# Row tile 0 of x loaded in two row halves on two queues, and one early weight piece moved to the other queue

## The chip, the cores and the metric

One core of a Trainium2 chip runs the program. The metric is the device time of one execution in microseconds (us); the profile's span is about 2 us shorter. Executions at the full granted TensorE clock (0.999 to 1.000) count as fast.

## The reference, cut to what matters

```python
x = A_x                                   # 1 x 2048 x 640, bf16
xn = layernorm(x)
s = attention(xn @ wq, last 512 keys and values of the caches) @ wo     # 32 heads of 192
g = silu((silu(xn @ w_gate) * (xn @ w_up)) @ w_down)                    # F = 1536
return x + s * g
```

Only the first operations matter here: the layer norm of the first row tiles (128 rows each) and their products with `w_gate` and `w_up`.

## The kernel before

The kernel begins with loads, while TensorE (PE) runs filler matmuls on zeros, meant to raise its clock. A row tile goes x, statistics (VectorE), root (ScalarE), normalise (VectorE), transpose (PE), evacuation (ScalarE), then matmuls with the first 384 columns of both weights. These columns come in four early pieces: gate piece 0 and up piece 0 (rows of contraction blocks 0 and 1, 192 KB each), gate piece 1 and up piece 1 (blocks 2 to 4, 288 KB each).

```python
def load_x(t, eng=nc.sync):
    x_t[t] = lnx.tile([P, D], bf, name="x_t")
    eng.dma_start(out=x_t[t][:], in_=x2[t * P : (t + 1) * P, :])

def load_first(cs):
    for w_sb, w in ((wg_sb, B_w_gate), (wu_sb, B_w_up)):
        src = w[cs.start * P : cs.stop * P, 0:FQ].rearrange("(c p) f -> p c f", p=P)
        nc.sync.dma_start(out=w_sb[:, cs, 0:FQ], in_=src)
...
load_x(0, nc.scalar)
load_x(1, nc.scalar)
load_first(slice(0, 2))
load_first(slice(2, NC))
nc.scalar.activation(act_t[:], one_t[:], ACT.Sqrt)     # brings the table load forward
load_x(2)
load_x(3)
load_gu(1)
load_gu(2)
...
keep_warm(9)          # filler: 9 matmuls of 512 columns
keep_warm(6, P)       # and 6 of 128
...
ln_stats(0)
ln_sqrt(0)
ln_stats(1, lambda: ln_apply(0, (slice(0, 2 * P), slice(2 * P, D))))
ready(0)              # transposes and evacuation of tile 0
...
if t == 0:            # tile 0: pieces 0 first, then gate piece 1, then up piece 1
    order = order[:12] + [(f, s, [c]) for s in range(2) for c in range(2, NC) for f in range(3)]
```

The softmax here doesn't subtract the row's maximum and nothing guards it: scores larger than these inputs give would overflow.

## Time and profile before

| | before |
|---|---|
| median of three executions | 920.98 us (920.62 to 921.85) |
| span of the profiled one | 919.2 us |
| PE busy | 913.1 us |
| statistics of x tile 0 begin | 3.70 us |
| transposes of tile 0 begin | 5.79 us |
| first useful matmul | 6.64 us |
| last early piece (up piece 1) has landed | 2.25 + 4.8 = 7.05 us |

Read it thus: PE is the bound from its first useful matmul on, so whatever this change does is decided before about 8 us. A landing is worked out here as the start of the issue plus the profile's time from issue to landing. The prediction below shows the lines.

For comparing starts I use one **mark**: the start of the first 128x512 gate matmul, when PE has finished the four single row tiles. In the kernel before it is here (start, length, engine, line, operation):

```profile
14.76 1.24 PE L279 MATMUL gu<-xnT,wg_sb 128*128 128x512 bf16 x4
```

### The profile page before, as it was taken

The numbers are of one execution on the slowest core, as the hardware profiler recorded it, in microseconds if no ns is written. First come the engines' busy times: TensorE is split into PE (matmuls) and PEld (weight loads), VectorE is DVE, ScalarE is ACT, GpSimd is POOL, SyncE is SP. The second block draws the span as 40 slices with busy tenths as digits, with TensorE's granted clock in tenths as the row PEclk, the third lists the DMA queues.
The fourth block names the chain that finished last, engine by engine and source line by source line (L and its number), as shares of the span: only waits on it lengthen the run. The fifth ranks groups of instructions, "written<-read, shape, count | busy, mean of one in ns | idle before, by whom it ended". The sixth has DMA issues, their size and how long they took to land.

```text
span 919.2 us, 23149 instructions
## 1 busy us (share of the span) xinstructions
PE 913.1 (99%) x9898; PEld 550.9 (60%) x9920; DVE 601.7 (65%) x844; ACT 474.5 (52%) x840; POOL 85.5 (9%) x269
## 2 busy tenths in 40 slices
PE   9999999999999999999999999999999999999998
PEld 6444444465757575756565666666666666665565
DVE  6443321467677777777777777676867777777657
ACT  4222222557464646565656565655555555556471
POOL 0000000000000000000000000000000000002976
PEclk9999999999999999999999999999999999999999
DMA  9312430045353534253534353435243544343526
GB/s 310 68 35 64 90 84 0 1 75 112 54 113 50 112 49 108 55 107 55 108 58 109 57 109 54 108 53 105 59 82 78 90 77 80 85 71 102 121 58 166
DMA packets 248150, 77.53 MB, mean 84 GB/s; under 512 B 228976, under 2 KB 248048, under 8 KB 248048
## 3 DMA queue, kind: packets, MB, share of 16 engines
q1 hardware_dynamic: 246032, 73.67, 39.3%
q10 hardware_dynamic: 2016, 2.39, 0.8%
q8 instruction: 77, 1.26, 0.6%
q14 instruction: 25, 0.20, 0.1%
HBM read 38.93 MB, written 2.62 MB: 45 GB/s over the span
## 4 chain that ended last, share of the span: by engine, by line
PE 99%; issue 0%; DVE 0%; ACT 0%
PE mm L447 22%; PE sc L461 18%; PE mm L486 16%; PE sc L601 15%; PE sc L279 11%; PE mm L309 6%; PE sc L571 4%; PE sc L563 2%; PE mm L538 2%; PE mm L563 1%; PE gu L227 1%; PE gu L279 0%; PE mm L318 0%; PE sc L486 0%; PE sc L538 0%
## 5 line engine op out<-in xcount | busy, mean ns | idle before, releaser
L465 ACT ACTIVATE p_t<-sc 128x1024 bf16<-128x1024 f32 x254 | 253.0, 1023 | 119.9 <-PE sc L461 119.9
L452 DVE TENSOR_REDUCE qT<-mm 128x512 bf16<-128x1024 f32 x189 | 231.1, 1223 | 99.0 <-PE mm L447 96.6
L516 ACT ACTIVATE O_b<-mm,r 128x192 bf16<-128x192 f32 x486 | 165.1, 422 | 183.7 <-issue 139.7
L447 PE MATMUL mm<-xnT,wq_p 64*128 64x512 bf16 x1890 | 237.7, 376 | 0.0
L461 PE MATMUL sc<-qT,khat 64*128 64x512 bf16 x1524 | 198.1, 376 | 0.0
L486 PEld LDWEIGHTS <-p_t 64*128 64x128 bf16 x3584 | 159.6, 93 | 33.6
L486 PE MATMUL mm<-V_p,p_t 64*128 64x193 bf16 x3520 | 176.8, 242 | 0.0
L614 DVE TENSOR_TENSOR s_m<-s_m,sc 128x1024 f32<-128x1024 f32 x108 | 131.9, 1221 | 60.4 <-PE sc L601 52.3
L601 PE MATMUL sc<-wo_p,OT_b 64*128 64x512 bf16 x1296 | 168.9, 376 | 0.0
L447 PEld LDWEIGHTS <-wq_p 64*128 64x128 bf16 x1890 | 105.8, 94 | 98.1 <-issue 0.8
L461 PEld LDWEIGHTS <-khat 64*128 64x128 bf16 x1536 | 85.9, 94 | 79.9 <-DVE s_t L614 0.3
L601 PEld LDWEIGHTS <-OT_b 64*128 64x128 bf16 x1296 | 70.5, 94 | 43.8 <-issue 0.3
L614 DVE TENSOR_TENSOR s_t<-s_t,sc 128x512 f32<-128x512 f32 x108 | 74.2, 687 | 28.4 <-PE sc L571 26.6
L588 POOL MEMSET turn_t<- 128x1 f32 x220 | 21.8, 99 | 700.0 <-PE mm L486 506.0
L287 DVE TENSOR_TENSOR hT<-sc,sg 128x512 bf16<-128x512 f32 x46 | 31.7, 692 | 81.6 <-ACT sg L286 81.6
L286 ACT ACTIVATE sg<-sc 128x512 bf16<-128x512 f32 x46 | 27.3, 597 | 69.8 <-PE sc L279 65.1
L279 PE MATMUL sc<-xnT,wg_sb 128*128 128x512 bf16 (+1 forms) x255 | 60.0, 354 | 0.4
L279 PE MATMUL sc<-xnT,wu_sb 128*128 128x512 bf16 (+1 forms) x255 | 59.5, 355 | 0.2
L571 PE MATMUL sc<-OT_b,wo_p 64*128 64x512 bf16 (+1 forms) x345 | 50.3, 376 | 0.0
L309 PE MATMUL mm<-wd_sb,hT 128*128 128x512 bf16 x189 | 43.6, 379 | 0.2
L279 PEld LDWEIGHTS <-wu_sb 128*128 128x128 bf16 x285 | 27.1, 98 | 26.9 <-issue 0.2
L279 PEld LDWEIGHTS <-wg_sb 128*128 128x128 bf16 x285 | 27.2, 98 | 26.4
(83 smaller groups left out, 418.1 us busy)
## 6 DMA issues: line engine op xcount, KB each, us to landing
wo_p<-in_A_wo_dram SPq DMA_DIRECT2D x16, 480.0 KB, 4.8
K_p<-in_A_k_cache_dram SPq DMA_DIRECT2D x32, 192.0 KB, 4.3
V_p<-in_A_v_cache_dram SPq DMA_DIRECT2D x32, 192.0 KB, 3.3
wq_p<-in_A_wq_dram SPq DMA_DIRECT2D x64, 80.0 KB, 2.9
wq_p<-in_A_wq_dram SPq DMA_DIRECT2D x16, 160.0 KB, 3.2
x_t<-in_A_x_dram SPq DMA_DIRECT2D x14, 160.0 KB, 2.8
x_b<-in_A_x_dram SPq DMA_DIRECT2D x4, 512.0 KB, 6.1
OT_b<-O_b SPq DMA_TRANSPOSE x124, 2.8
```

Of the source, the lines that this page charges most:

```text
L279: nc.tensor.matmul(out, w_sb[:, c, f * P : (f + 1) * P], xnT[:, c, qc], start=(c == 0), stop=(c == NC - 1),)
L287: nc.vector.tensor_tensor(hTs[b][:, f, :], u, sg[:], ALU.mult)
L309: nc.tensor.matmul(dn, at, by, start=(f == 0), stop=(f == NF - 1))
L447: nc.tensor.matmul(q_ps[:, h, :], pairs[pr]["wq"][r, c, j * P : (j + 1) * P], xnT[r, c, b * 512 : (b + 1) * 512], start=(c == 0), stop=(c ...
L452: nc.vector.reduce_sum(qTs[i][:, j, :], q_ps[:, :, :].rearrange("p h n -> p n h"), axis=AX.X)
L461: nc.tensor.matmul(sc[:, h, :], khat[r, j, ks], qT[r, j, :], start=(j == 0), stop=(j == 2))
L465: nc.scalar.activation(p_t[:, :, :], sc[:, :, :], ACT.Exp, scale=scale)
L486: m = nc.tensor.matmul(acc[:, k, h * 256 : h * 256 + Dh + 1], Ps[i][kc][r, h, qt * P : (qt + 1) * P], V_p[r, kc, h, 0 : Dh + 1], start=(p ...
L516: nc.scalar.activation(O_b[:, qt, h, :], a_k[:, h, 0:Dh], ACT.Copy, scale=r[:, k, h, :])
L571: nc.tensor.matmul(ps.rearrange("p (t q) -> p t q", q=P), pairs[i // NB]["wo"][r, j, MC:D], OTs[i][:, :, :].rearrange("p (t j) q -> p j t ...
L601: m = nc.tensor.matmul(ps[:, k, :], OTs[i][r, 3 * (2 * half + k) + j, :], pairs[i // NB]["wo"][r, j, MAIN], start=(turn == 0 and j == 0), ...
L614: nc.vector.tensor_tensor(to, to, ps, ALU.add)
```

## The change

The intent: row tile 0, which everything waits for at the start, should land earlier if each queue carries half of its rows. To relieve SyncE's queue of what it now carries, up piece 1 goes to ScalarE's queue, ahead of the Sqrt table load.

```diff
-        def load_x(t, eng=nc.sync):
+        def load_x(t, engs=(nc.sync,)):
             x_t[t] = lnx.tile([P, D], bf, name="x_t")
-            eng.dma_start(out=x_t[t][:], in_=x2[t * P : (t + 1) * P, :])
+            n = P // len(engs)
+            for k, eng in enumerate(engs):
+                r = slice(k * n, (k + 1) * n)
+                eng.dma_start(out=x_t[t][r, :], in_=x2[t * P + r.start : t * P + r.stop, :])
...
-                nc.sync.dma_start(out=w_sb[:, cs, 0:FQ], in_=src)
+                eng.dma_start(out=w_sb[:, cs, 0:FQ], in_=src)
...
-        load_x(0, nc.scalar)
-        load_x(1, nc.scalar)
+        load_x(0, (nc.scalar, nc.sync))
+        load_x(1, (nc.scalar,))
         load_first(slice(0, 2))
-        load_first(slice(2, NC))
+        load_first(slice(2, NC), (nc.sync, nc.scalar))
```

More of the change, by code (lines that the diff above doesn't have):

```diff
@@ L181, with load_first @@
         x_t, ln, xns = {}, {}, {}
-        def load_x(t, eng=nc.sync):
+        def load_x(t, engs=(nc.sync,)):
             x_t[t] = lnx.tile([P, D], bf, name="x_t")
-            eng.dma_start(out=x_t[t][:], in_=x2[t * P : (t + 1) * P, :])
-        def load_first(cs):
-            for w_sb, w in ((wg_sb, B_w_gate), (wu_sb, B_w_up)):
+            n = P // len(engs)
+            for k, eng in enumerate(engs):
+                r = slice(k * n, (k + 1) * n)
+                eng.dma_start(out=x_t[t][r, :], in_=x2[t * P + r.start : t * P + r.stop, :])
+        def load_first(cs, engs=(nc.sync, nc.sync)):
+            for w_sb, w, eng in zip((wg_sb, wu_sb), (B_w_gate, B_w_up), engs):
                 src = w[cs.start * P : cs.stop * P, 0:FQ].rearrange("(c p) f -> p c f", p=P)
-                nc.sync.dma_start(out=w_sb[:, cs, 0:FQ], in_=src)
+                eng.dma_start(out=w_sb[:, cs, 0:FQ], in_=src)
         def load_gu(q):
```

## The prediction

> **What bounds the kernel now.** I read the page first, then busy time by stretch, then the start in order of time, then the packets of the two DMA queues. The page says that TensorE (PE) is the bound.
>
> ```profile
> span 919.2 us, 23149 instructions
> PE 913.1 (99%) x9898; PEld 550.9 (60%) x9920; DVE 601.7 (65%) x844; ACT 474.5 (52%) x840; POOL 85.5 (9%) x269
> PE 99%; issue 0%; DVE 0%; ACT 0%
> ```
>
> Only 6.1 us of the 919.2 have no matmul in flight, and the chain that ended last runs along PE alone. So a change counts only if it lets PE begin its real work earlier or takes a gap out of its stream. The table of stretches says where such time lies (columns: stretch, length, then busy us and count of PE, PEld, DVE, ACT, POOL, the clock, DMA share, GB/s):
>
> ```profile
> 0.00:20.00 20.00, 18.66 (x179) 12.67 (x181) 12.02 (x36) 9.24 (x20) 0.79 (x8) 1.00 0.97 304
> 20.00:100.00 80.00, 79.63 (x365) 36.22 (x371) 33.52 (x70) 20.90 (x35) 3.81 (x6) 1.00 0.29 66
> 900.00:919.20 19.20, 15.50 (x100) 9.43 (x98) 13.50 (x24) 1.53 (x5) 11.76 (x9) 0.98 0.64 183
> ```
>
> The change touches the first ten microseconds only. There PE is idle 20.00 - 18.66 = 1.34 us, of which 1.23 us pass before its first instruction. But "busy" covers filler: 15 matmuls on zeros. The timeline of the start shows when real work begins:
>
> ```profile
> 0.71 0.91 ACTq L185 DMA_DIRECT2D x_t<-in_A_x_dram  x2
> 0.72 0.46 SPq L190 DMA_DIRECT2D wg_sb<-in_B_w_gate_dram  x1
> 1.66 1.28 ACT L205 ACT_TABLE_LOAD   x1 [1.66 <-PEq L841]
> 3.70 0.89 DVE L240 BATCH_NORM_STATS2 stats<-x_t 128x6 f32<-128x320 bf16 x2 [2.52 <-DMA x_t<-in_A_x_dram]
> 4.75 0.44 DVE L240 BATCH_NORM_STATS2 stats<-x_t 128x6 f32<-128x320 bf16 x1
> 5.19 0.16 DVE L262 RECIPROCAL rstd<-rstd 128x1 f32<-128x1 f32 x1
> 5.39 0.34 DVE L264 TENSOR_SCALAR xn<-x_t,mv,rstd 128x256 bf16<-128x256 bf16 x1
> 5.58 0.31 PE L227 MATMUL gu<-zero_t 128*128 128x128 bf16 x1
> 5.79 0.13 PEld L332 LDWEIGHTS <-xn 128*128 128x128 bf16 x2 [0.17 <-DVE xn L264]
> 6.22 0.37 ACT L338 COPY xnT<-tp 128x256 bf16<-128x256 bf16 x1 [1.06 <-PE tp L332]
> 6.64 0.27 PE L279 MATMUL sc<-xnT,wg_sb 128*128 128x128 bf16 x1
> ```
>
> The reader is to see one chain: row tile 0 of x lands at 3.70, VectorE sums it, ScalarE takes the root, VectorE normalises, and PE transposes at 5.79 after a wait of 0.17 for xn. The evacuation follows at 6.22 and the first useful matmul at 6.64. The last filler matmul starts at 5.58. Fillers of this shape are spaced 0.11 us (5.47 to 5.58), so PE would be free at 5.69: **the late x costs PE only 5.79 - 5.69 = 0.10 us.** That is the figure on which everything below turns.
>
> **What the Trainium skill says.** (1) "DMA: Bandwidth & Descriptors", Rules for kernel authors, advises against two transfers to disjoint partition halves: both halves use all 16 DMA engines and share them. The same page, Issuing engines are not separate DMA queues, says a second issuing engine saves only issue time. The trace agrees for a loaded machine (about 340 to 370 GB/s from 2.8 us on, whichever queue the packets are from), but not for the first half microsecond: between 1.8 and 2.2 us ScalarE's queue (q10) moved only 134 to 138 GB/s with its engines shown 88 to 100% occupied, and the rate rose when the other queue (q1) joined. (2) "ScalarE: Activation LUTs", What ACT_TABLE_LOAD costs, gives about 1.28 us per load plus a drain; the trace has 1.28 us, and the next ACTIVATE follows at 2.95, so no drain shows. (3) "TensorE: Matmul & The Clock Gate", Part 1, says that the array starts at half clock and goes to full only after some microseconds of activity, in a free-running window. The trace agrees: small matmuls are 0.11 us apart until about 7.0 us and 0.055 us after.
>
> **The change part by part.** *Row tile 0 in two halves.* Before, 160 KB go on q10. Both ScalarE loads make 288 packets in this window, so 144 a tile. The counts per 0.2 us from 1.6 are 5, 21, 21, 25, 25, 18, 20, 25: 144 is reached near 3.1 us, and the tile lands (issue 0.71 + 3.0) at 3.70. A half is 72 packets, and q10 reached 5 + 21 + 21 + 25 = 72 at 2.4 us. The other half leads on q1, whose first packets came near 2.1 us; at q10's 25 per 0.2 us it ends near 2.7. With the same 0.6 us from last packet to landing, x lands between 3.0 and 3.4 (an estimate): **0.3 to 0.7 us earlier.**
>
> *Row tile 1.* It matters because VectorE runs in order, and one statistics half of tile 1 (4.75 to 5.19) stands ahead of the reciprocal of tile 0. It lands at 1.17 + 3.4 = 4.57 now. It follows 72 packets in place of 144, so I expect 4.0 to 4.4. The reciprocal then starts near 4.5 to 4.9, and the first part of xn is ready 0.20 + 0.34 us later, at 5.0 to 5.4. That is before 5.69, so **the filler becomes the limit**, and only 0.10 of the 0.3 to 0.7 us reaches PE.
>
> *What 0.10 us at the transposes is worth.* First useful matmul at 6.54 in place of 6.64. But the clock rises near 7.0 us by its own window, and before that a matmul takes 0.11 in place of 0.055 us. If that instant stays, the 0.10 us hold one slow matmul more and save one fast one: 0.055 us. If it moves along: 0.10. I take 0.08 us.
>
> *SyncE's queue starts one x half (some 0.46 us of issue) later.* Gate piece 0 lands at 0.72 + 3.4 = 4.1 and would land near 4.5; up piece 0 at 1.24 + 3.9 = 5.1, then 5.5 to 5.9; both are first used at 6.6. Gate piece 1 lands at 1.74 + 4.4 = 6.1; all early bytes (320 KB of x, 960 KB of weights) are in at 7.05 now, so even as the last of them it comes by about 7.05, and its first weight load is at 7.44 (7.34 if all moves up). Hidden, with a margin of 0.3 us in the worst case.
>
> *The last up piece on ScalarE's queue.* Lands at 2.25 + 4.8 = 7.05 now, first used at 7.94. Issued near 1.6 it lands near 6 to 6.6. Already hidden: nothing gained, nothing lost.
>
> *Table load.* Three issues of some 0.44 us from 0.71 end near 2.1 in place of 1.62, so load and dummy Sqrt end near 3.65 in place of 3.15. The first real Sqrt is at 4.86, perhaps 4.3 afterwards. Hidden.
>
> *x tiles 2 and 3.* Same five issues ahead of tile 3 on SyncE, so about the same landing (7.5 and 7.9) against their use at 7.89 and 8.93.
>
> Sum: -0.08 us of 921.
>
> **The rivals.** (a) The split brings nothing because both halves share engines, as the first page says: 0.0 us. For it: the full rate later on. Against it: the slow first half microsecond. (b) A weight becomes PE's wait, because the weights now share the engines with twice as many queues: gate piece 1 past 7.35 would cost 0.1 to 0.5 us, so 921.1 to 921.5. For it: DMA share is 1.0 from 3 us on. Against: the margins above; I give it one in seven. (c) The whole chain moves up: if the clock rises during the filler, the filler ends early, and x sets PE's start with all its 0.3 to 0.7 us: 920.3 to 920.7. This trace has the filler slow to its end; one in seven. (d) A later consumer gives the gain back: the ScalarE evacuations leave only gaps of 0.1 us (10.79 to 10.97), and these move with PE, so I don't expect it.
>
> **Range and chances.** Centre 920.98 - 0.08 = 920.9 us. The three runs before span 920.62 to 921.85, so the scatter of 1.2 us is fifteen times the effect; the clock's free phase could make such scatter, which this one trace can't show. Range 920.0 to 921.8. A change by 2% is 18.4 us, more than twice all that lies before the first useful matmul: faster 0.005, same 0.99, slower 0.005.
>
> **What would show it.** Right: the first statistics start at 3.0 to 3.4; the wait of PEld for xn at the first transposes is gone and they start at 5.69; first useful matmul near 6.54; later matmuls in the same spacing; table load near 2.1. Wrong: the statistics still at 3.6 or later (rival a); weight loads on wg_sb waiting for a DMA near 7.4 (rival b); fillers at 0.055 us before 5.5 (rival c). The number fails if the executions of the new kernel fall on another part of the scatter than those of the old one.

## The result, and the profile after

The changed kernel takes 921.21 us (median of 6, 920.99 to 921.87); the kernel before, run beside it, 921.25 us (median of 6, 920.62 to 922.26). The ratio is 0.9999 with a 95% interval of 0.9986 to 1.0012: the same. (The ratio is the mean time of the one kernel's fast runs over that of the other's in the same rounds, so not quite the ratio of the medians.)

The page's lines, and the table of stretches:

```profile
span 919.0 us, 23151 instructions
PE 99%; DMA 1%; SPq 0%; issue 0%; DVE 0%
0.00:20.00 20.00, 18.45 (x179) 12.14 (x181) 12.19 (x36) 9.21 (x20) 0.79 (x8) 1.00 0.95 297
20.00:100.00 80.00, 79.63 (x366) 36.29 (x371) 33.52 (x70) 20.90 (x35) 3.81 (x6) 1.00 0.30 68
```

After 20 us nothing changed: 79.63 us of PE busy in the second stretch, as before. Before 20 us PE is busy 0.21 us *less* (18.45 against 18.66) although the mark comes 0.08 us earlier. And the chain that ended last, which was PE to the start before, now holds DMA. The timeline of the start, with the same instructions as in the prediction:

```profile
0.72 0.60 SPq L188 DMA_DIRECT2D x_t<-in_A_x_dram  x1
0.72 1.20 ACTq L188 DMA_DIRECT2D x_t<-in_A_x_dram  x2
1.38 0.81 SPq L193 DMA_DIRECT2D wg_sb<-in_B_w_gate_dram  x1
2.24 0.45 SPq L193 DMA_DIRECT2D wu_sb<-in_B_w_up_dram  x1
2.43 1.28 ACT L208 ACT_TABLE_LOAD   x1 [2.43 <-issue]
3.42 0.89 DVE L243 BATCH_NORM_STATS2 stats<-x_t 128x6 f32<-128x320 bf16 x2 [2.24 <-DMA x_t<-in_A_x_dram]
5.51 0.63 PE L335 MATMUL tp<-ident,xn 128*128 128x128 bf16 x5
6.26 0.22 PE L282 MATMUL sc<-xnT,wg_sb 128*128 128x128 bf16 x1
6.54 0.10 PEld L282 LDWEIGHTS <-wu_sb 128*128 128x128 bf16 x1 [0.52 <-DMA wu_sb<-in_B_w_up_dram]
7.40 0.28 PEld L282 LDWEIGHTS <-wg_sb 128*128 128x128 bf16 x5 [0.25 <-DMA wg_sb<-in_B_w_gate_dram]
```

The statistics of x begin 0.28 us earlier, the transposes start 0.28 us earlier, the first useful matmul 0.38 us earlier. Then PE stops twice: for up piece 0, and for gate piece 1. (The weight loads wait 0.52 and 0.25 us; the starts of the matmuls around them are 0.28 and 0.30 us apart in place of 0.055, so PE itself loses 0.23 and 0.24.) Neither wait exists in the kernel before, where SyncE issues these two pieces 1.00 us earlier, at 1.24 and 1.74 in place of 2.24 and 2.74:

```profile
1.24 0.46 SPq L190 DMA_DIRECT2D wu_sb<-in_B_w_up_dram  x1
1.74 0.46 SPq L190 DMA_DIRECT2D wg_sb<-in_B_w_gate_dram  x1
```

From issue to landing (the last number, us; first the kernel before, then the changed one) they take 0.4 and 0.2 us longer:

```profile
wu_sb<-in_B_w_up_dram SPq DMA_DIRECT2D x1, 192.0 KB, 3.9
wg_sb<-in_B_w_gate_dram SPq DMA_DIRECT2D x1, 288.0 KB, 4.4
```

```profile
wu_sb<-in_B_w_up_dram SPq DMA_DIRECT2D x1, 192.0 KB, 4.3
wg_sb<-in_B_w_gate_dram SPq DMA_DIRECT2D x1, 288.0 KB, 4.6
```

The chain of the changed kernel's execution names the second wait as the one that counts: a transfer issued at 2.74 ends PE's wait at 7.41.

```profile
2.24 0.45 SPq L193
2.69 0.04 issue
2.74 4.62 DMA wg_sb<-in_B_w_gate_dram
7.36 0.05 issue
7.41 0.28 PE sc L282 x2
```

Part of the early start is not of the change at all. In this execution the clock rose near 5.1 us (from there the fillers start 0.056 us apart in place of 0.107), so the filler ended early; in the profiled execution of the kernel before it rose near 7.0.

### The profile page after: what moved, and what is told of

Same layout as the page of the kernel before. It is cut to its first block, busy times and chain, and to the rows that moved or that the text cites. A ratio compares the mean times of both kernels' runs of the same rounds, so it can differ in the third digit from the quotient of the medians.

```text
span 919.0 us, 23151 instructions
## 1 busy us (share of the span) xinstructions
PE 912.8 (99%) x9898; PEld 548.4 (60%) x9920; DVE 601.6 (65%) x844; ACT 474.4 (52%) x840; POOL 85.5 (9%) x269
## 4 chain that ended last, share of the span: by engine, by line
PE 99%; DMA 1%; SPq 0%; issue 0%; DVE 0%
PE mm L450 22%; PE sc L464 18%; PE mm L489 16%; PE sc L604 15%; PE sc L282 11%; PE mm L312 6%; PE sc L574 4%; PE sc L566 2%; PE mm L541 2%; PE mm L566 1%; DMA wg_sb<-in_B_w_gate_dram 1%; PE gu L282 0%; PE mm L321 0%; PE sc L541 0%; PE sc L489 0%
```

## The experiments

Twelve runs, on several chips. A look is one execution with its profile; each line gives the statistics of tile 0 ("x"), the landings of up 0, gate 1 and up 1, the sum of weight loads' waits for transfers, and the mark.

| run | x | up 0 | gate 1 | up 1 | waits | mark |
|---|---|---|---|---|---|---|
| before, first look | 3.70 | 5.1 | 6.1 | 7.05 | 0 | 14.76 |
| b_again | 3.60 | 4.9 | 6.55 | 7.35 | 0 | 14.53 |
| b_third | 3.66 | 5.2 | 6.15 | 7.05 | 0 | 14.44 |
| after, first look | 3.42 | 6.5 | 7.35 | 5.85 | 0.77 | 14.68 |
| a_again | 3.47 | 6.35 | 7.55 | 5.75 | 0.9 | 14.88 |
| split_only | 3.44 | 6.15 | 7.95 | 8.8 | 1.0 | 15.93 |
| move_only | 3.79 | 5.2 | 7.85 | 6.95 | 0.6 | 15.17 |
| halves_act | 5.78 | 4.6 | 6.85 | 7.85 | 0 | 16.57 |
| cols_split | 3.08 | 7.3 | 8.2 | 7.5 | 1.9 | 15.52 |
| up_act | 3.41 | 5.95 | 8.6 | 9.0 | 1.2 | 15.94 |
| up_act_whole | 3.53 | 7.55 | 5.6 | 8.8 | 1.1 | 15.52 |
| cols_only | 3.00 | 5.2 | 6.1 | 7.6 | 0.2 | 14.85 |
| cols_f8 | 3.12 | 5.2 | 6.1 | 7.4 | 0 | 14.54 |
| cols_x2 | 2.97 | 5.6 | 7.4 | 8.2 | 0.3 | 14.99 |

One caution on the landings. The packed trace holds sixteen completion signals for each load, and the profile's landing is the last of them. In the five looks at the two kernels themselves, the last signal of an early weight piece comes at most 0.24 us after the fifteenth. In five of the other looks it comes 0.4 to 1.2 us after it, and there the fifteenth came before PE needed the piece (needed: 0.055 us after the start of the last matmul before it; all in us):

| look | piece waited for | 15th signal | last signal | needed |
|---|---|---|---|---|
| split_only | gate 1 | 6.93 | 7.92 | 7.24 |
| up_act | gate 1 | 7.42 | 8.60 | 7.47 |
| up_act_whole | up 0 | 6.47 | 7.55 | 6.89 |
| cols_only | up 1 | 7.18 | 7.62 | 7.44 |
| cols_x2 | up 1 | 7.36 | 8.18 | 7.94 |

So these waits hang on one signal of sixteen in a single look. Whether its lag belongs to the program or to the execution is not shown. Where it matters I also give the eighth signal, by which half of the signals are in.

The theory at the outset: x is early as intended, and its half on SyncE's queue delays the weights behind it. The rival: the moved up piece takes the bandwidth from them.

### Both kernels again: what belongs to an execution

No edit.

> The kernel before, unchanged, for a second look at what differs between executions of one program. If the TensorE clock rises at an instant that belongs to the execution (free window), the spacing of the filler matmuls falls from 0.11 to 0.055 us at another time than near 7.0 us. Landings should repeat: row tile 0 summed from 3.6 to 3.8, no weight load waits for a DMA, first useful matmul 6.4 to 6.7. If instead the early clock belongs to the changed kernel, this run rises near 7.0 again.

> The changed kernel, unchanged. If its two waits for weights (0.52 us for up piece 0, 0.25 us for gate piece 1) belong to the program, they are here again within 0.2 us each, the statistics of tile 0 start at 3.3 to 3.6, and the transposes of tile 1 start at 8.0 to 8.2. If they were an accident of that execution, no weight load waits for a DMA and those transposes start before 7.8.

> A third look at the kernel before, to know the scatter of its start. As in the first two looks: x summed at 3.5 to 3.8, no weight load waits for a transfer, the clock rises anywhere between 4.5 and 7.1 us, the mark at 14.4 to 14.9, later with a later rise.

The waits belong to the program: a_again has both, and neither further look at the kernel before has any. Their sizes moved by more than the 0.2 us forecast, though (gate piece 1: 0.58 us against 0.25). From a_again's list of waits (engine, line, what it waited for, us in all, times, longest):

```profile
PEld L282 <- DMA wg_sb<-in_B_w_gate_dram: 0.6, 1, 0.6
PEld L282 <- DMA wu_sb<-in_B_w_up_dram: 0.3, 1, 0.3
```

The clock does not. A 128x128 matmul is recorded at 0.31 us while the clock is low and at 0.22 when it is up. In the kernel before, first look, they fall to 0.22 near 7.1 us; in b_again the last filler, at 5.58, is already at 0.24, and in b_third the clock is up before that. A late rise goes with a mark 0.2 to 0.3 us later in the kernel before (14.76 against 14.53 and 14.44). So the first-look comparison, 14.76 to 14.68, sets a late clock against an early one. **Where both had an early clock, the changed kernel's mark is later, by 0.15 to 0.44 us** (14.68 and 14.88 against 14.53 and 14.44). Against b_third the sum closes within 0.02 us: the first useful matmul comes 0.24 and 0.20 us earlier (6.26 and 6.30 against 6.50), PE then loses 0.47 and 0.62 us to the two waits, and the mark is 0.24 and 0.44 us later. Four looks are few, and the size is not settled. The time cannot help: all 28 executions of the kernel before in this study average 921.16 us, the 7 of the changed one 921.33, with standard deviations of 0.46 and 0.36 us.

### One part at a time

split_only:

```diff
-        load_first(slice(2, NC), (nc.sync, nc.scalar))
+        load_first(slice(2, NC))
```

> Tile 0 in halves on the two queues, last up piece left on SyncE. Theory (the half on SyncE's queue delays the weights behind it): up piece 0 is waited for again, by 0.3 to 0.6 us, and x is summed at 3.3 to 3.5. Rival (the moved up piece takes bandwidth from the weights): no wait for up piece 0 and gate piece 1, as the moved piece is away. In either case the last up piece lands later than in the changed kernel.

move_only:

```diff
-        load_x(0, (nc.scalar, nc.sync))
+        load_x(0, (nc.scalar,))
```

> Tile 0 whole on ScalarE's queue, last up piece moved there. Theory (the half on SyncE is the cause): SyncE issues its first gate piece at 0.72 and up piece 0 at 1.24 as in the kernel before, no weight load waits, x is summed at 3.6 to 3.8, first useful matmul at 6.5 to 6.7. Rival (the moved piece is the cause): a wait of 0.2 us or more for up piece 0 or gate piece 1.

Neither the theory nor its rival holds alone: **each part by itself makes gate piece 1 late**, at 7.95 with the split alone and 7.85 with the move alone, against 6.1 to 6.55 before. So say the eighth signals too: 6.22 and 6.68, against 5.51 to 5.82 before and 6.79 and 7.04 with both parts. From the issue to that signal it is 3.47 us with the split alone, 4.93 with the move alone, 3.77 to 4.07 before, and 4.05 and 4.30 with both (one or two looks each, three before). So the split delays the piece by its later issue, and the move alone by a longer transfer; in the changed kernel the later issue, 1.00 us, is most of it. With the split alone, up piece 0 was not waited for (it landed at 6.15, and this execution's late clock put its first use at 6.57), so that expectation missed. Gate 1, up 1 and x tile 2 were waited for instead (gate 1 through its last signal alone, see the caution above), and its single time was 922.35 us beside 920.96 for the kernel before. With the move alone SyncE issues as early as before, and still:

```profile
PEld L282 <- DMA wg_sb<-in_B_w_gate_dram: 0.6, 1, 0.6
```

Here up piece 1 no longer comes after gate piece 1 but beside it, on the other queue, and the x tiles behind move up. By the landings one would say that, given the split, the move helps (gate piece 1 at 7.35 and 7.55 with it, 7.95 without). By the eighth signals it is the reverse (6.79 and 7.04 with it, 6.22 without), so that is not shown.

The table of stretches for the first 5 us shows a lower rate besides (the last column is GB/s). The kernel before comes first, then the changed one, then split_only.

```profile
0.00:5.00 5.00, 3.77 (x9) 1.34 (x10) 1.63 (x7) 1.62 (x3) 0.79 (x8) 1.00 0.64 194
```

```profile
0.00:5.00 5.00, 3.77 (x9) 1.34 (x10) 1.91 (x8) 1.78 (x3) 0.79 (x8) 1.00 0.56 170
```

```profile
0.00:5.00 5.00, 3.77 (x9) 1.34 (x10) 1.89 (x8) 1.78 (x3) 0.79 (x8) 1.00 0.54 143
```

194 against 170 and 143 GB/s over 5 us is 970 against 850 and 715 KB: less had arrived. The changed kernel's first data come later too: none before 2.0 us, in both looks, where the kernel before had moved 27 to 34 KB by then in its three. But this rate does not decide whether a weight is late: in the same 5 us move_only moved 184 GB/s with a wait of 0.6 us, b_third 185 with none, and cols_only (below) 175 with gate piece 1 in at 6.1.

### Is it the shape of the halves?

halves_act (both 64-row halves on ScalarE, all weights on SyncE):

```diff
-        load_x(0, (nc.scalar, nc.sync))
+        load_x(0, (nc.scalar, nc.scalar))
-        load_first(slice(2, NC), (nc.sync, nc.scalar))
+        load_first(slice(2, NC))
```

> Both 64-row halves of tile 0 issued by ScalarE one after the other, nothing of x on SyncE, all four weight pieces on SyncE as in the kernel before. Theory (a 64-row load is slow to issue whoever else is issuing): each half takes 0.55 us or more on ScalarE, and the first data of that queue come at 2.0 us as in the changed kernel. Rival (the two queues get in each other's way when both begin with x): each half takes 0.45 us or less and first data come at 1.7. If SyncE's first two pieces again take 0.46 us each, the lengthening of SyncE's gate piece 0 to 0.82 us came from the x half ahead of it.

cols_split (the changed kernel, but halves of 320 columns and all 128 rows):

```diff
-            n = P // len(engs)
+            n = D // len(engs)
             for k, eng in enumerate(engs):
-                r = slice(k * n, (k + 1) * n)
-                eng.dma_start(out=x_t[t][r, :], in_=x2[t * P + r.start : t * P + r.stop, :])
+                c = slice(k * n, (k + 1) * n)
+                eng.dma_start(out=x_t[t][:, c], in_=x2[t * P : (t + 1) * P, c])
```

> The changed kernel with tile 0 halved by columns (128 rows of 640 bytes on each queue) in place of rows. Theory (the 64-row shape is what issues slowly): the x halves issue in 0.45 us or less, SyncE reaches up piece 0 near 1.75 in place of 2.24, it lands near 5.9, no wait or one under 0.2 us for it. Rival (any first transfer on both queues is slow): issues of 0.55 us or more and the wait of 0.3 to 0.5 us again. Twice the packets of half the size could also make x land later, 3.5 to 3.8.

The issues on ScalarE's queue in halves_act (two halves and tile 1):

```profile
0.72 1.84 ACTq L188 DMA_DIRECT2D x_t<-in_A_x_dram  x3
```

And SyncE's first two in cols_split, with the statistics:

```profile
0.72 0.41 SPq L188 DMA_DIRECT2D x_t<-in_A_x_dram  x1
1.18 0.44 SPq L193 DMA_DIRECT2D wg_sb<-in_B_w_gate_dram  x1
3.08 0.89 DVE L243 BATCH_NORM_STATS2 stats<-x_t 128x6 f32<-128x320 bf16 x2 [1.90 <-DMA x_t<-in_A_x_dram]
```

**The slow issue comes from the shape.** A load of 64 rows takes 0.56 to 0.61 us to issue on whichever queue, and what follows it is slow too: ScalarE's three took 1.84 us in all with no x on SyncE, whose first two pieces kept their 0.47 and 0.45 us, and in the changed kernel the gate piece behind SyncE's half takes 0.81 us. A load of 128 rows and half the columns takes 0.41 us and leaves the next at 0.44. With columns the statistics of x begin at 3.08, another 0.34 us earlier than with rows. In halves_act the statistics begin 2.1 us later than in the kernel before and the span is 1.7 us longer, which also shows that the start passes to the end. Why the second half there took 4.4 us from issue to landing is not shown.

But the earlier x did not help cols_split: up piece 0 issued near 1.7, as expected, yet landed at 7.3 and not near 5.9, and the weight load waited 1.6 us for it. The last signal lagged by 0.8 us here, but the fifteenth, at 6.42, was late as well (needed near 5.97). So the row shape is one cause and not the whole.

### Another order for the weights

up_act moves up piece 0 to ScalarE as well; up_act_whole does so with tile 0 whole on ScalarE.

```diff
-        load_first(slice(0, 2))
+        load_first(slice(0, 2), (nc.sync, nc.scalar))
```

```diff
-        load_x(0, (nc.scalar, nc.sync))
+        load_x(0, (nc.scalar,))
-        load_first(slice(0, 2))
+        load_first(slice(0, 2), (nc.sync, nc.scalar))
```

> The changed kernel with up piece 0 on ScalarE's queue as well: SyncE x half, gate 0, gate 1; ScalarE x half, x tile 1, up 0, up 1, then the table load near 2.9. Theory (a weight is late because of what stands ahead of it in its queue): up piece 0 issues at 1.95 and lands near 5.6 to 6.0, gate piece 1 issues at 2.24 and lands near 6.8, so the waits for both fall to 0.2 us or less in sum and the tile 1 transposes start at 7.5 to 7.9. Rival (total bandwidth limits, order does not matter): the sum of waits stays at 0.6 us or more, on whichever piece is last.

> Tile 0 whole on ScalarE, both up pieces behind x on ScalarE's queue, gate pieces and then x tiles 2 and 3 on SyncE. Theory (sharing by queue: whatever is second in a queue waits for that queue alone): gate piece 1 lands earlier than with the up piece 0 ahead of it, by 6.3; up 0 lands near 6, up 1 near 7.3; no wait or one under 0.2 us; x is summed at 3.6 to 3.8, transposes of tile 1 at 7.7 to 8.2. Rival (bandwidth): waits of 0.5 us or more on up pieces.

Both theories missed; the rival's sums (1.2 and 1.1 us of waits) came true. But both waits are of the kind in the caution above: by the fifteenth signal there would have been none. In up_act gate piece 1 was issued at 2.24, half a microsecond sooner than in the changed kernel, and landed about 1.1 us later, although its eighth signal came sooner (6.32 against 6.79 and 7.04). So neither the theory nor the rival is settled. In up_act_whole gate piece 1 was early (5.6) and both up pieces late (7.55 and 8.8). My reading, which is not shown, is that a weight moved to the second queue does not go to the front: what stood behind it on the first queue moves up and shares the stream. No run separates this from the mere sharing of the two queues. Of the six looks with an up piece on ScalarE's queue, none was without a wait for weights. Some pieces take 6 us and more from issue, when the counted bytes of all early loads were in well before. The lag of the last signal is part of that (1.17 us of 6.35 for gate piece 1 in up_act); why it lags I could not settle.

### A version with what was learnt

cols_only: column halves, and all weights on SyncE as in the kernel before. cols_f8: one filler matmul less besides. cols_x2: cols_only with x tile 2 on ScalarE.

```diff
-        load_first(slice(2, NC), (nc.sync, nc.scalar))      # on top of cols_split
+        load_first(slice(2, NC))
```

```diff
-        keep_warm(9)                                        # cols_f8, on top of cols_only
+        keep_warm(8)
```

```diff
+        load_x(2, (nc.scalar,))                             # cols_x2: right after load_x(1, ...)
-        load_x(2)
```

> Tile 0 in column halves on the two queues, all four weight pieces on SyncE as in the kernel before: the version that should keep the early x and lose the late weights. Theory (the row shape and the moved piece make the weights late, not the early x): x is summed at 3.0 to 3.3; gate 1 issues at 2.19 and lands at 6.6 to 7.0, up 1 at 7.3 to 7.8; the waits of weight loads for transfers come to under 0.4 us (0.8 and 0.9 in the two looks at the changed kernel), and the first 128x512 gate matmul, a mark that has followed the span within 0.15 us in all looks so far, starts at 14.2 to 14.6 (before 14.5 to 14.8). Time: 0.1 to 0.5 us under the kernel before, which timing cannot tell from nothing. Rival (the bytes themselves bind: 1280 KB must be in before the row tile is done, so an earlier x only lengthens the wait for weights): mark at 14.6 or later with waits of 0.5 us or more.

> The same with one 512-column filler matmul less (8 in place of 9), so that the filler ends near 5.26 at half clock. Theory (the filler limits once x is early): transposes start at 5.1 to 5.3, and the mark comes up to 0.3 us earlier than with 9, if the weights are in. Rival (weights bind): the waits of weight loads grow by what the transposes gained, 0.3 to 0.4 us, and the mark stays within 0.1 us of the version with 9.

> Column halves of tile 0, weights on SyncE, and x tile 2 moved from behind the weights to ScalarE's queue behind tile 1. In the look without this move, tile 2 landed at 8.1 and PE waited 0.23 us for its xn at the tile 2 transposes. Theory (the early transfers are one stream of some 340 GB/s, and a load moved forward delays those it passes): tile 2 lands by 6.5 and no longer delays PE, but the weights lose 160 KB, about 0.45 us: up 1 lands at 7.8 to 8.2 in place of 7.6 and PE waits 0.3 to 0.7 us for weights; the mark stays within 0.3 us of 14.85. Rival (tile 2 was the last obstacle): waits for weights stay at 0.2 us, the mark comes at 14.5 or earlier. Time: unchanged within 0.1 per cent in both.

In cols_only the weights are hardly late (0.2 us of waits) and the statistics of x begin 0.6 to 0.7 us earlier than in the kernel before. It differs from split_only by the shape of the halves alone, and there its gain shows: gate piece 1 is issued at 2.18 in place of 2.75, its eighth signal comes at 5.85 in place of 6.22, and the mark at 14.85 in place of 15.93 (one look each, and split_only's last signal is part of the difference). Yet the mark is 14.85, outside both forecasts, because the wait moved on. The chain names x tile 2, from its issue at 3.22 to 8.10, and PE's transposes of that tile wait for its xn:

```profile
3.22 4.87 DMA x_t<-in_A_x_dram
...
8.12 0.90 DVE stats L243 x2
```

```profile
10.31 0.45 PE L335 MATMUL tp<-ident,xn 128*128 128x128 bf16 x5 [0.23 <-DVE xn L267]
```

The last signal counts here too: the fifteenth of tile 2 came at 7.61. cols_x2 brings tile 2 forward, and now up piece 1 lands at 8.2 in place of 7.6 and is waited for by 0.3 us, as forecast, but by one late signal (the fifteenth came at 7.36, against 7.18 in cols_only): mark 14.99, though part of that is a late clock in this execution. cols_f8 did what its theory said, transposes at 5.26 and a mark 0.31 us before cols_only's, and with that came back to where the kernel before lies (14.54). Times: cols_only 921.38 us (median of 5), ratio 1.0005 (0.9991 to 1.0019); cols_x2 921.14, ratio 0.9998 (0.9984 to 1.0012); cols_f8 once, 920.69. **No version is shown to beat the kernel before.** Each time a load came earlier, a later load became the wait, in cols_only and cols_x2 by its last signal.

## Why the prediction was right or wrong

The number was right: 920.9 us with a range of 920.0 to 921.8 was forecast, 921.21 was measured, and "same" with it. For the most part this is because the whole start is small beside the span, so the right number says little for the steps; that they came out to nothing is in part luck. Taken one by one:

- **PE sets the time, and only its start can change.** Right. The stretch after 20 us did not move, and span minus mark is constant within 0.2 us over 14 executions.
- **x lands 0.3 to 0.7 us earlier, at 3.0 to 3.4.** Just missed at the slow end: 3.42 and 3.47, so 0.13 to 0.28 earlier than in the three looks before, which also answers rival (a). The estimate left out that 64-row halves issue more slowly and that first data come only at 2.0 us. With column halves the landing was where I put it (2.97 to 3.12).
- **The filler becomes the limit, and the transposes start at 5.69.** Right where the clock rose late: 5.68 in split_only, up_act and cols_x2. In the changed kernel's own looks an early clock ended the filler sooner, and they began at 5.51 and 5.56. That is rival (c), and it is a matter of the execution.
- **SyncE's weights come some 0.46 us later, and stay hidden.** This is the step that failed. Up piece 0 was to land at 5.5 to 5.9 and landed at 6.5 and 6.35; gate piece 1 was to be in by about 7.05 even at worst, and came at 7.35 and 7.55. The mis-sized term is the delay: both pieces are issued 1.00 us later (2.24 against 1.24, 2.74 against 1.74), not 0.46, because the half takes 0.60 us to issue and the gate piece after it 0.81 in place of 0.46. The bound for gate piece 1 failed because it took all early loads to be in before what was issued after them. They were not: by 7.0 us the changed kernel had moved about 1520 KB (850 by 5 us, then 296 and 375), more than all early loads together, and gate piece 1 was still out. The clock had its part as well. It rose early and brought PE's need forward to 6.3 and 7.2 us; at the uses that I had counted on, 6.6 and 7.44, the first look's landings would have been just in time. So rival (b), which I gave one in seven, is in both looks.
- **The last up piece on ScalarE: nothing gained, nothing lost.** Wrong as told. It landed earlier than forecast (5.75 and 5.85, not 6 to 6.6), and alone it delays gate piece 1 by 1.3 us or more, with a wait of 0.6 us (one look).
- **x tiles 2 and 3 land as before (7.5 and 7.9).** Wrong by 0.36 us: 7.82 and 8.29. In neither look at the changed kernel did PE wait for them.
- **Table load hidden.** Right: 2.43 to 3.71, with the first real root at 4.58, though it began later than the 2.1 forecast.
- **Sum of -0.08 us.** Not borne out, and not refuted by the time. The marks of like clock say later by 0.15 to 0.44 us. The mechanism, an early x and then two new waits for weights, is shown by the chain, by a repeat and by the sum that closes against b_third; the net size over many executions is not.

## What to carry to other kernels

When a first load is late, ask what the next four loads have as slack before spending bandwidth or issue time on it: here there was 0.1 us of PE's wait for x to win, while in the three looks before up piece 0 had 1.4 to 1.6 us to spare, gate piece 1 0.6 to 1.4 and up piece 1 0.25 to 1.0, and the change took 0.8 to 1.5 us from the first two. If such a tile is to be halved, halve it along its columns, with all its rows: that issued in 0.41 us in place of 0.60. And leave a piece in its place in the queue if it is on time: in every look with an up piece on the second queue some weight came late (in up_act and up_act_whole by one late signal). Look at more than one execution before you name a load as the cause: a landing can hang on one signal of sixteen.

## What the Trainium skill lacked or had wrong

- "DMA: Bandwidth & Descriptors", Rules for kernel authors, says of halves of the partitions that they are not worth it because they share engines. The outcome agrees (no gain in time), though no run here tests that cause: the halves did bring x forward (3.42 and 3.47 against 3.60 to 3.70), and what they cost was slow issuing, 0.56 to 0.61 us for 64 rows against 0.41 for 128 rows of half the columns, with 0.81 for the load behind. I found no page that gives an issue time by row count.
- The same page, Issuing engines are not separate DMA queues, says that issuing from several engines saves only issue time. It has no figure for what it can cost: one up piece moved to the second queue, with nothing else changed, brought gate piece 1 from 6.1-6.55 to 7.85 us (one look).
- "TensorE: Matmul & The Clock Gate", Part 1, calls the window free-running and puts the rise of the clock at about 4 us of activity, plus or minus 0.5. Here the fillers begin at 1.23 us, and the rise came between about 3.9 us (move_only) and 7.1 us (the first look before), so 2.7 to 5.9 us after: a wider spread, though in the late case PE had paused for up to 0.3 us on the way. (A note in the same Part does say that the number of slow matmuls changes from run to run.) It goes with some 0.3 us of the mark, as much as the change itself.
- I found no page that gives a figure for how far the last of a load's completion signals can fall behind on loads from SyncE's and ScalarE's queues. Here it came 0.4 to 1.2 us after the fifteenth in the five looks of the table, and at most 0.24 us after it in the five looks at the two kernels.
